# Loading x in 128-partition halves: one padded transfer in place of 112 partitions and a last row

## The chip, the cores and the metric

The kernel runs on one core of one Trainium2 chip. Time is the device time of one execution in microseconds (us). The engines are TensorE (PE; its weight loads are shown as PEld), VectorE (DVE), ScalarE (ACT), GpSimd (POOL) and SyncE (SP). SP computes nothing: in this kernel it issues nearly all transfers between device memory and SBUF, in the order in which its program lists them, and 16 DMA engines carry them out.

## What is computed

```python
def _attn_ref(x, filt_r, filt_i):            # x: 8 x 3136 x 256
    X = np.fft.rfft(x, axis=1)
    F = (filt_r + 1j * filt_i)[None, :, :]
    return np.fft.irfft(X * F, n=x.shape[1], axis=1)
def _moe_ref(x, w_gate, w1, w2, capacity):   # x: what _attn_ref gave; capacity 128
    scores = np.einsum('bsd,d->bs', x, w_gate)
    out = x.copy()
    for b in range(B):
        top_idx = np.argpartition(-scores[b], capacity)[:capacity]
        xe = x[b, top_idx]
        ye = np.maximum(xe @ w1, 0.0) @ w2
        g = 1.0 / (1.0 + np.exp(-scores[b, top_idx]))
        out[b, top_idx] = xe + g[:, None] * ye
```

Each of the 8 batches is filtered along its 3136 positions in the frequency domain; the 128 positions of each batch with the highest scores then get a small feed-forward network.

## The kernel before

The Fourier transforms are matmuls: 3136 = 98 x 32, and the 98 rows are cut in two groups of 49 (`NH`). A batch lies in the SBUF tile `X` (partitions x 2 channel halves x 2 x 16 x 128 floats): group 0 in partitions 0 to 48, group 1 in partitions 64 to 112. So 113 partitions hold data or the zeros between the groups, each with 16 KB in one channel half. All compute on `X` works on `64 + NH` = 113 partitions.

`X` is one buffer for all batches, and its life in the steady state is a cycle. `fold` (L489, on POOL or DVE) makes sum and difference of the two middle indices, or the sum is left to PE; `amm` (L500, on PE) multiplies; `tout` (L505, DVE) transposes the product into `UU`. `inner` then filters the batch (L376 to L441). When batch t+1 has been consumed from `X`, the results of batch t-1 are written into the same place by `join` (L541) or `yout` (L567), `store_rows` (L579, L580) sends that half to device memory in six transfers, and `load` (L594, L595) brings that half of batch t+2 in. A load thus has to wait until the six stores of its half have been read out, and the folds of the next batch wait for the load.

`load` is called for 14 halves (batches 1 to 7), and issues two transfers for each: first the row of partition 112, 16 KB cut in 16 pieces (L594), then partitions 0 to 111 (L595). `load_first` does the same for batch 0, in four quarters with 8 KB in a partition (L608, L609). The host lays x out for that: per batch the 112 rows of both halves one behind the other, then the last rows.

The order of all work is written out as a list of numbers (`ORDER`), and every engine runs its part in that order; SP's part is the order of transfers. The transfers of SP go round eight completion semaphores ("lanes"), so a transfer may be issued only when the one eight places earlier has landed.

Of the kernel before, what the change touches and what calls it, by code (L numbers as in the profile page):

```python
# [18 lines left out]
B, S, D, FF = 8, 3136, 256, 1024  # L19
N1, N2, K2, L, LP = 98, 32, 32, 25, 32  # L20
NH, NG = 49, 16
# [233 lines left out]
def kernel(  # L255
# [7 lines left out]
    nc = tc.nc  # L263
# [61 lines left out]
    def op(when, eng, cost, fn, r=(), w=(), new=None, lat=0.0, bias=0.0, sooner=0.0, mode=0, tag=None):  # L325

        prog.append((when, len(prog), eng, cost, fn, r, w, new, (tag or fn.__name__, *where)))
# [129 lines left out]
    halves = [c_sb[:, _COLS["wi"].start + NH * k:_COLS["wi"].start + NH * k + 64] for k in range(2)]  # L457
# [121 lines left out]
                nc.sync.dma_start(out=oi[b, g, :48, h, :, d], in_=X[64 * g:64 * g + 48, x, h])  # L579
            nc.sync.dma_start(out=oi[b, :, 48, h, :, d], in_=X[48::64, x, h])  # L580

    XM = 2 * 112 * 4096

    def load(when, b, h, xy, bias=0.0):
        n = NCH // 2
        where[:] = "ld", b, h
        if b < B:
            keys = [("x", h, c, g) for c in range(h * n, h * n + n) for g in range(2)]
            to = X[:, h].rearrange("p k n d -> p (k n d)")
            main = x[b, :XM].rearrange("(h p e) -> h p e", h=2, p=112)  # L590
            ends = x[b, XM:].rearrange("(r h e) -> h r e", h=2, r=16)

            def fetch():
                nc.sync.dma_start(out=to[112:113].rearrange("p (r e) -> p r e", r=16), in_=ends[h:h + 1])  # L594
                nc.sync.dma_start(out=to[:112], in_=main[h])  # L595

            op(when, "sp", 7.15, fetch, [], keys, lat=2.2, bias=bias, tag="load")

    x_flat = X.rearrange("p x k n d -> p (x k n d)")
    x_first = x_flat.rearrange("p (q k n d) -> p q k n d", q=4, k=2, n=NG)  # L600

    def load_first():
        main = x[0, :XM].rearrange("(q p e) -> q p e", q=4, p=112)
        ends = x[0, XM:].rearrange("(r q e) -> q r e", q=4, r=16)

        def quarter(q):
            to = x_flat[:, 2048 * q:2048 * q + 2048]
            nc.sync.dma_start(out=to[112:113].rearrange("p (r e) -> p r e", r=16), in_=ends[q:q + 1])  # L608
            nc.sync.dma_start(out=to[:112], in_=main[q])  # L609

        for q in range(4):
            keys = [("x", q // 2, 4 * q + c, g) for c in range(4) for g in range(2)]
            op(XQ[q], "sp", 3.7, lambda q=q: quarter(q), [], keys, lat=2)
# [528 lines left out]
    if WARM:  # L1142
        op(-99.5, "pe", .117 * WARM, warmup, (), (), new=("y", "warm"))
        for _ in range(FILL):
            op(-99.4, "pe", .64, fill, (), [("y", "warm")])
    op(-99, "sp", .4, lambda: nc.sync.dma_start(out=c_sb[:, :192], in_=cst[:, :192]), (), ["wa"], lat=2)
    load_first()
    for k, (a, e) in enumerate(((0, 4 * CUT), (4 * CUT, L))):
        op(TFT[k], "sp", .25 + .125 * (e - a), lambda a=a, e=e: nc.sync.dma_start(out=tf_sb[:, a:e], in_=tf.rearrange("p (l c) -> p l c", c=64)[:, a:e]),
# [34 lines left out]
    for h in range(2):  # L1184
        load(TS + TC0 * NCH / 2 * (h + 1) + 1, 1, h, xys[1], XA)
    for t in range(B + 1):
        T0 = t * P if t < B else (B - 1) * P + C8
        if t < B:
            if t == 0:
                inner(I0, P - I0, t)  # L1190
            else:
                inner(T0, P if t < B - 1 else P7, t)
        co, tc_ = (CO, TCO) if t < B - 1 else (C7, TC7) if t == B - 1 else (0, .95)
        outer(T0 + co, tc_, t - 1, t + 1, xys[t + 1])
        if t + 2 < B + 2:
            for h in range(2):
                load(T0 + co + tc_ * NCH / 2 * (h + 1) + (6 if t < B - 1 else 4), t + 2, h, xys[t + 2])
        if t >= 1:
            select(T0 + SO if t < B else T0 - C8 + S7, t - 1, sts[t - 1])
# [45 lines left out]
```

## Time and profile before

| | |
|---|---|
| median of 3 runs | 459.41 us (453.93 to 1026.87) |
| profiled execution | 455.47 us |
| its span (first to last instruction) | 453.7 us |
| PE busy | 416.2 us (92%) |
| DVE busy | 355.8 us (78%) |
| POOL busy | 328.2 us (72%) |
| ACT busy | 313.0 us (69%) |
| DMA, mean over the span | 152 GB/s |
| granted TensorE clock, mean | 0.972 |

The rows further down are from the profiled execution. Busy time of PE is that of overlapping matmuls, so 92% does not say that it runs at its peak. "L595" is line 595 of the kernel. `<-` in a pair of names reads "written from". A number in square brackets with `<-` behind an instruction is the time its engine sat idle before it and what ended that.

### The profile page before, as it was taken

Reading aid. Unit: us, or ns where it says so; the run is one execution under the profiler, and the core shown is the slowest. Engines: PE = TensorE matmul, PEld = TensorE weight load, DVE = VectorE, ACT = ScalarE, POOL = GpSimd, SP = SyncE. Lnnn points to the kernel's source line nnn. Section 1 sums busy time; section 2 is a strip of 40 time slices with the busy share of each in tenths; the row PEclk is TensorE's granted clock in tenths of the full one; section 3 lists DMA queues with packets and bytes.
Section 4 is the critical chain, followed back from the end, with each engine's and each line's share of the span. In section 5 each row is a group of like instructions: output and inputs, shape, how many; then the busy total and the mean of one; then the engine's idle time right before and its main releaser. Section 6 shows DMA issues by size and latency. Waiting matters only on the chain.

```text
span 453.7 us, 13314 instructions
## 1 busy us (share of the span) xinstructions
PE 416.2 (92%) x5348; PEld 249.7 (55%) x5348; DVE 355.8 (78%) x711; ACT 313.0 (69%) x798; POOL 328.2 (72%) x215
## 2 busy tenths in 40 slices
PE   9999999999699998979999799989999979998884
PEld 9644565545354644535555454456545756577773
DVE  2568899989869898995889698979899985964421
ACT  1429947789268977984989397948988997852210
POOL 2317799797969588867998589539889995964121
PEclk9999999999889999997999899989999989999999
DMA  8999973058654757584747563675253791566100
GB/s 230 256 258 277 243 175 92 8 138 226 163 124 111 207 136 201 144 211 110 212 103 196 152 200 91 183 183 161 63 125 96 181 267 27 131 154 151 39 25 35
DMA packets 61548, 69.05 MB, mean 152 GB/s; under 512 B 4014, under 2 KB 57550, under 8 KB 59214
## 3 DMA queue, kind: packets, MB, share of 16 engines
q1 hardware_dynamic: 60718, 66.10, 57.0%
q0 software_dynamic: 768, 2.10, 1.5%
q8 instruction: 42, 0.69, 0.6%
q14 instruction: 20, 0.16, 0.1%
HBM read 41.27 MB, written 26.91 MB: 150 GB/s over the span
## 4 chain that ended last, share of the span: by engine, by line
PE 42%; DMA 18%; DVE 15%; POOL 10%; ACT 9%; issue 4%; SPq 1%; POOLq 0%; ACTq 0%; DVEq 0%
DMA X<-in_x_dram 9%; PE pv L500 4%; DVE t L479 4%; ACT junk L441 4%; POOL q L435 3%; DMA fb_sb<-in_fri_dram 3%; PE pv L1006 3%; DVE y L384 3%; POOL xh L489 3%; PE py L400 3%; PE pa L500 3%; DMA out_dram<-X 2%; DVE q L391 2%; PE pa L1034 2%; DVE UU L505 2%
## 5 line engine op out<-in xcount | busy, mean ns | idle before, releaser
L435 POOL TENSOR_TENSOR q<-UU,wg_sb 128x1024 f32<-128x1024 f32 (+1 forms) x47 | 109.1, 2327 | 11.7 <-ACT UU L408 5.0
L541 POOL TENSOR_TENSOR X<-xh,X 113x512 f32<-113x512 f32 x64 | 81.7, 1287 | 18.5 <-ACT X L537 14.1
L441 ACT ACTIVATE junk<-q 128x256 bf16<-128x256 f32 x180 | 75.1, 417 | 13.2 <-POOL q L435 8.1
L479 DVE STREAM_TRANSPOSE t<-UU 128x1024 f32<-128x1024 f32 x64 | 78.0, 1224 | 0.0
L489 POOL TENSOR_TENSOR xh<-X 113x512 f32<-113x512 f32 x26 | 34.7, 1341 | 24.1 <-DMA X<-in_x_dram 24.1
L387 POOL TENSOR_TENSOR q<-q,fb_sb 128x1024 f32<-128x1024 f32 (+1 forms) x18 | 40.6, 2254 | 11.9 <-ACT q L380 11.7
L489 POOL TENSOR_TENSOR X<-X 113x512 f32<-113x512 f32 x24 | 31.2, 1302 | 13.2 <-DMA fa_sb<-in_fri_dram 7.0
L500 PE MATMUL pv<-X,c_sb 49*64 49x512 f32 x184 | 33.7, 709 | 7.1 <-DMA X<-in_x_dram 4.0
L441 ACT ACTIVATION_READ_ACCUMULATOR junk<-q 128x1 f32 x180 | 33.9, 188 | 0.0
L726 ACT ACTIVATE junk<-R,nb 128x392 bf16<-128x392 f32 (+1 forms) x48 | 30.0, 626 | 4.9 <-DVE nb L747 4.2
L505 DVE STREAM_TRANSPOSE UU<-pv 128x1024 f32<-128x1024 f32 x19 | 23.6, 1240 | 10.0 <-PE pv L500 9.9
L500 PE MATMUL pa<-X,c_sb 49*64 49x512 f32 x192 | 30.0, 596 | 0.5 <-DVE UU L505 0.5
L505 DVE STREAM_TRANSPOSE UU<-pa 128x1024 f32<-128x1024 f32 x21 | 25.9, 1233 | 5.4 <-PE pa L500 5.4
L1018 ACT ACTIVATE q<-pv 128x384 fp32r<-128x384 f32 (+2 forms) x18 | 8.0, 457 | 29.8 <-PE pv L1006 21.3
L1020 DVE SCALAR_TENSOR_TENSOR y<-pv,q 128x384 fp32r<-128x384 f32 (+2 forms) x18 | 9.0, 511 | 24.3 <-ACT q L1018 19.3
L384 DVE TENSOR_TENSOR y<-pa,fa_sb 128x1024 f32<-128x1024 f32 (+1 forms) x19 | 22.5, 1186 | 3.8 <-PE pa L376 2.9
L500 PE MATMUL py<-X,c_sb 49*64 49x512 f32 x168 | 24.0, 592 | 0.0
L563 PE MATMUL pz<-t,c_sb 64*64 64x512 f32 x160 | 23.1, 618 | 0.5 <-ACT X L567 0.5
L400 PE MATMUL py<-y,ti_sb 64*64 64x256 f32 x252 | 21.7, 396 | 0.7 <-DVE y L384 0.7
L376 PE MATMUL pa<-UU,tf_sb 64*64 64x256 f32 x292 | 21.2, 395 | 0.9 <-DMA tf_sb<-in_tf_dram 0.2
L400 PE MATMUL py<-q,ti_sb 64*64 64x256 f32 x252 | 21.1, 386 | 0.0
L1046 POOL DMA_INDIRECT out_dram<-fb_sb,idx_sb x6 | 5.9, 980 | 20.3 <-DVE fb_sb L1042 12.9
(340 smaller groups left out, 1144.8 us busy)
## 6 DMA issues: line engine op xcount, KB each, us to landing
X<-in_x_dram SPq DMA_DIRECT2D x14, 1792.0 KB
out_dram<-X SPq DMA_DIRECT2D x64, 384.0 KB
X<-in_x_dram SPq DMA_DIRECT2D x4, 896.0 KB
R<-scr SPq DMA_DIRECT2D x14, 196.0 KB
fb_sb<-in_moe_w_dram SPq DMA_DIRECT2D x2, 1024.0 KB
fa_sb<-in_fri_dram SPq DMA_DIRECT2D x4, 256.0 KB
fb_sb<-in_fri_dram SPq DMA_DIRECT2D x4, 256.0 KB
ti_sb<-in_ti_dram SPq DMA_DIRECT2D x1, 576.0 KB
```

What stands on the lines that cost most here:

```text
L384: nc.vector.tensor_tensor(out=wide(y), in0=wide(h["z"]), in1=filt(fa_sb), op=ALU.mult)
L387: nc.gpsimd.tensor_tensor(out=wide(h["q"]), in0=wide(h["q"]), in1=filt(fb_sb), op=ALU.mult)
L400: nc.tensor.matmul(v[o, j, c], lhsT=ti_at[p, k, 2 * i + e, hi], rhs=y[p, hi, c], start=k == 0, stop=k == 1)
L435: nc.gpsimd.tensor_tensor(out=h["q"][:, e0:e0 + ne].rearrange("p e (j d) -> p e j d", j=2), in0=u.rearrange("p e d j -> p e j d"), in1=wg_ ...
L441: nc.scalar.activation(out=rk, in_=h["q"][:, e, j * D:j * D + D], func=AF.Copy, accum_out=urow(b, ls[2 * e + j], D, DS))
L479: nc.vector.transpose(out=h["t"].rearrange("p d (l j) -> p d l j", j=2), in_=uchan(b_out, c))
L489: eng.tensor_tensor(out=(area(1) if k else h["f"])[:64 + NH], in0=area(0)[:64 + NH], in1=area(1)[:64 + NH], op=(ALU.add, ALU.subtract)[k])
L500: nc.tensor.matmul(ap[64 * k:64 * k + 64, g].rearrange("p (n d) -> p n d", d=DW), lhsT=todo[k][i][0][p], rhs=todo[k][i][1][p], start=i == ...
L505: nc.vector.transpose(out=uchan(b_in, c), in_=a.rearrange("p (l j) d -> p d l j", j=2))
L541: eng.tensor_tensor(out=area(k)[:64 + NH], in0=h["e"][:64 + NH], in1=odd, op=(ALU.add, ALU.subtract)[k])
L563: nc.tensor.matmul(h["y"][64 * g:64 * g + 64, k], lhsT=halves[k][p], rhs=h["t"][p, :, NG * g:NG * g + NG], start=turn == 0, stop=turn == 1)
L726: nc.scalar.activation(out=junk, in_=st["R"][:, ph], func=AF.Sign, bias=st["nb"], accum_out=cnt)
```

## The change

x is laid out by the host with 128 partitions for each half of a batch (partitions 49 to 63 and 113 to 127 are zeros), and each half is fetched by one transfer of 128 partitions x 16 KB. Batch 0's quarters likewise are one transfer of 128 partitions x 8 KB. No compute instruction changes; `X` already had 128 partitions, of which the last 15 were not written before and are not read afterwards.

```diff
-    XM = 2 * 112 * 4096
-
     def load(when, b, h, xy, bias=0.0):
...
-            main = x[b, :XM].rearrange("(h p e) -> h p e", h=2, p=112)
-            ends = x[b, XM:].rearrange("(r h e) -> h r e", h=2, r=16)
+            main = x[b].rearrange("(h p e) -> h p e", h=2, p=128)

             def fetch():
-                nc.sync.dma_start(out=to[112:113].rearrange("p (r e) -> p r e", r=16), in_=ends[h:h + 1])
-                nc.sync.dma_start(out=to[:112], in_=main[h])
+                nc.sync.dma_start(out=to, in_=main[h])
...
     def load_first():
-        main = x[0, :XM].rearrange("(q p e) -> q p e", q=4, p=112)
-        ends = x[0, XM:].rearrange("(r q e) -> q r e", q=4, r=16)
+        main = x[0].rearrange("(q p e) -> q p e", q=4, p=128)

         def quarter(q):
-            to = x_flat[:, 2048 * q:2048 * q + 2048]
-            nc.sync.dma_start(out=to[112:113].rearrange("p (r e) -> p r e", r=16), in_=ends[q:q + 1])
-            nc.sync.dma_start(out=to[:112], in_=main[q])
+            nc.sync.dma_start(out=x_flat[:, 2048 * q:2048 * q + 2048], in_=main[q])
...
-    padded = np.zeros((B, 2, 64 + NH, 4096), np.float32)
-    padded[:, :, :NH], padded[:, :, 64:] = halves[:, :, 0], halves[:, :, 1]
...
+    padded = np.zeros((B, 2, 128, 4096), np.float32)
+    padded[:, :, :NH], padded[:, :, 64:64 + NH] = halves[:, :, 0], halves[:, :, 1]
```

Only SP's program changes. Here is SP in the steady state, from the stores of one half of batch 0 to the load of batch 3 that takes their place, before. `DMAHW0` to `DMAHW7` are the eight lanes; a wait on a compute engine's name is a wait for its work.

```order
L579 DMA out_dram<-X 48x16x128 [waits DMAHW2_49,DVE_49,DMAHW3_49,Activation_49,Pool_49]
L579 DMA out_dram<-X 48x16x128
L580 DMA out_dram<-X 32x1x128 [waits DMAHW4_49]
L579 DMA out_dram<-X 48x16x128 [waits DMAHW5_49,Pool_49]
L579 DMA out_dram<-X 48x16x128 [waits DMAHW6_49]
L580 DMA out_dram<-X 32x1x128
L594 DMA X<-in_x_dram 1x16x256 [waits DMAHW4_49,DMAHW7_49,DMAHW0_49,PE_49]
L595 DMA X<-in_x_dram 112x4096 [waits DMAHW5_49,DMAHW3_49,DMAHW6_49,DMAHW2_49,DMAHW1_49]
```

And the same place in the changed kernel:

```order
L579 DMA out_dram<-X 48x16x128 [waits DMAHW2_49,DVE_49,DMAHW4_49,Activation_49,Pool_49]
L579 DMA out_dram<-X 48x16x128
L580 DMA out_dram<-X 32x1x128
L579 DMA out_dram<-X 48x16x128 [waits DMAHW5_49,Pool_49]
L579 DMA out_dram<-X 48x16x128 [waits DMAHW6_49]
L580 DMA out_dram<-X 32x1x128
L591 DMA X<-in_x_dram 128x4096 [waits DMAHW4_49,DMAHW5_49,DMAHW3_49,DMAHW6_49,DMAHW2_49,DMAHW7_49,DMAHW0_49,PE_49]
```

The two transfers, of which the first waited for the short stores (L580) and the second for the long ones (L579), are one that waits for all six. The other place is SP near the start, where batch 1's second half and batch 2's first are fetched behind the filter's tables, before:

```order
L1149 DMA tf_sb<-in_tf_dram 128x1088 [waits DMAHW2_49]
L1151 DMA wg_sb<-in_moe_w_gate_dram 128x256 [waits DMAHW3_49]
L1100 DMA fa_sb<-in_fri_dram 32x1536 [waits DMAHW4_49]
L1100 DMA fa_sb<-in_fri_dram 32x1536 [waits DMAHW5_49]
L1100 DMA fb_sb<-in_fri_dram 32x1536 [waits DMAHW6_49]
L1100 DMA fb_sb<-in_fri_dram 32x1536 [waits DMAHW7_49]
L594 DMA X<-in_x_dram 1x16x256 [waits DMAHW0_49,PE_49,Pool_49]
L595 DMA X<-in_x_dram 112x4096 [waits DMAHW1_49]
L594 DMA X<-in_x_dram 1x16x256 [waits DMAHW2_49,PE_49,Pool_49]
L595 DMA X<-in_x_dram 112x4096 [waits DMAHW3_49]
```

And in the changed kernel (its lines 1093, 1142 and 1144 are 1100, 1149 and 1151 of before):

```order
L1142 DMA tf_sb<-in_tf_dram 128x1088 [waits DMAHW5_49]
L1144 DMA wg_sb<-in_moe_w_gate_dram 128x256 [waits DMAHW6_49]
L1093 DMA fa_sb<-in_fri_dram 32x1536 [waits DMAHW7_49]
L1093 DMA fa_sb<-in_fri_dram 32x1536 [waits DMAHW0_49]
L1093 DMA fb_sb<-in_fri_dram 32x1536 [waits DMAHW1_49]
L1093 DMA fb_sb<-in_fri_dram 32x1536 [waits DMAHW2_49]
L591 DMA X<-in_x_dram 128x4096 [waits DMAHW3_49,PE_49,Pool_49]
L591 DMA X<-in_x_dram 128x4096 [waits DMAHW4_49,PE_49,Pool_49]
```

The order of the transfers stays; the small ones drop out, so the lane that each transfer waits for is that of another predecessor.

## Rows read from the trace of the kernel before

**Rows 1.** The page's chain that ended last, by engine and the first lines.
```profile
PE 42%; DMA 18%; DVE 15%; POOL 10%; ACT 9%; issue 4%; SPq 1%; POOLq 0%; ACTq 0%; DVEq 0%
```

**Rows 2.** The chain in order of time: start us, us, what.
```profile
40.43 13.90 DMA X<-in_x_dram
...
144.53 6.12 DMA out_dram<-X
...
150.71 9.13 DMA X<-in_x_dram
...
192.75 0.60 SPq L594
...
193.53 9.98 DMA X<-in_x_dram
203.65 3.66 PE pv L500 x14
...
288.38 9.65 DMA X<-in_x_dram
298.16 2.95 PE pv L500 x16
```

**Rows 3.** DMA issues: names, engine, count, KB of each.
```profile
X<-in_x_dram SPq DMA_DIRECT2D x14, 1792.0 KB
X<-in_x_dram SPq DMA_DIRECT2D x4, 896.0 KB
fb_sb<-in_moe_w_dram SPq DMA_DIRECT2D x2, 1024.0 KB
X<-in_x_dram SPq DMA_DIRECT2D x14, 16.0 KB
X<-in_x_dram SPq DMA_DIRECT2D x4, 8.0 KB
```

**Rows 4.** Windows: stretch, busy us (x instructions) of each engine, clock, DMA share, GB/s.
```profile
25.00:54.00 29.00, 28.43 (x384) 15.21 (x376) 24.13 (x28) 19.49 (x24) 16.55 (x10) 1.00 1.01 257
153.00:157.00 4.00, 4.00 (x70) 2.69 (x64) 4.00 (x6) 3.16 (x11) 3.92 (x3) 1.00 1.03 307
195.00:200.00 5.00, 4.72 (x72) 2.22 (x64) 4.87 (x15) 4.87 (x14) 2.93 (x2) 1.00 0.90 272
290.00:295.00 5.00, 4.46 (x76) 2.30 (x72) 4.93 (x15) 4.84 (x18) 2.57 (x2) 1.00 1.00 279
345.50:347.50 2.00, 1.96 (x36) 1.04 (x35) 1.89 (x9) 1.97 (x5) 1.92 (x3) 1.00 0.99 406
```

**Rows 5.** Timeline of SP: start us, us of the issue, line and names.
```profile
150.71 0.35 SPq L595 DMA_DIRECT2D X<-in_x_dram  x1
192.75 0.60 SPq L594 DMA_DIRECT2D X<-in_x_dram  x1
193.53 0.44 SPq L595 DMA_DIRECT2D X<-in_x_dram  x1
287.60 0.59 SPq L594 DMA_DIRECT2D X<-in_x_dram  x1
288.38 1.09 SPq L595 DMA_DIRECT2D X<-in_x_dram  x1
343.45 0.42 SPq L923 DMA_DIRECT2D fb_sb<-in_moe_w_dram  x1
```

**Rows 6.** Timeline of POOL, then PE: instructions that waited for a load [idle us <-releaser].
```profile
111.78 1.30 POOL L489 TENSOR_TENSOR xh<-X 113x512 f32<-113x512 f32 x1 [1.81 <-DMA X<-in_x_dram]
159.97 1.27 POOL L489 TENSOR_TENSOR xh<-X 113x512 f32<-113x512 f32 x1 [2.97 <-DMA X<-in_x_dram]
253.15 1.28 POOL L489 TENSOR_TENSOR xh<-X 113x512 f32<-113x512 f32 x1 [4.17 <-DMA X<-in_x_dram]
54.46 0.66 PE L500 MATMUL pz<-X,c_sb 49*64 49x512 f32 x4 [0.48 <-DMA X<-in_x_dram]
203.65 1.13 PE L500 MATMUL pv<-X,c_sb 49*64 49x512 f32 x4 [2.11 <-DMA X<-in_x_dram]
298.16 1.24 PE L500 MATMUL pv<-X,c_sb 49*64 49x512 f32 x8 [1.88 <-DMA X<-in_x_dram]
```

More of the change, by code (lines that the diff above doesn't have):

```diff
@@ L1226 @@
     halves = rows_of.reshape(B, 2, NH, 2, NG, 2, D // 2).transpose(0, 5, 1, 2, 3, 4, 6).reshape(B, 2, 2, NH, 4096)
-    padded = np.zeros((B, 2, 64 + NH, 4096), np.float32)
-    padded[:, :, :NH], padded[:, :, 64:] = halves[:, :, 0], halves[:, :, 1]
-    first = padded[0].reshape(2, 64 + NH, 2, NG, 2, 64).transpose(0, 4, 1, 2, 3, 5).reshape(4, 64 + NH, 2048)
-    data["x"] = np.concatenate([padded[:, :, :112].reshape(B, -1), padded[:, :, 112].reshape(B, 2, 16, 256).transpose(0, 2, 1, 3).reshape(B, -1)], 1)
-    data["x"][0] = np.concatenate([first[:, :112].reshape(-1), first[:, 112].reshape(4, 16, 128).transpose(1, 0, 2).reshape(-1)])
+    padded = np.zeros((B, 2, 128, 4096), np.float32)
+    padded[:, :, :NH], padded[:, :, 64:64 + NH] = halves[:, :, 0], halves[:, :, 1]
+    data["x"] = padded.reshape(B, -1).copy()
+    data["x"][0] = padded[0].reshape(2, 128, 2, NG, 2, 64).transpose(0, 4, 1, 2, 3, 5).reshape(-1)
     data.update(fri=np.stack([np.asarray(inputs[f"filt_{x}"])[rows].reshape(64, NPR, 2, D) for x in "ri"]), tf=tf.reshape(128, -1), ti=ti, cst=cst)
```

## Prediction

> **What bounds the kernel now.** I read the chain that ended last first. No engine owns it: PE has 42%, and transfers have 18%, more than DVE or POOL [rows 1]. The reader should see that a kernel whose PE is 92% busy still stands still for transfers. Then I took the chain in order of time to find which transfers those are. Loads of x stand in it four times, with 13.90, 9.13, 9.98 and 9.65 us from issue to landing [rows 2], together 42.66 us. They have two surroundings. The first, at 40.43, lies in the head of the program, where the tables and the first batches come in and the DMA engines are full (share 1.01 from 25 to 54 us, [rows 4]); its 13.90 us are mostly a queue. The other three are in the steady state: stores of a half end, SP issues the load that takes their place, and PE or POOL waits for it. I then asked the timelines who waits: PE sat idle 2.11 us before 203.65 and 1.88 us before 298.16, POOL 2.97 us before 159.97 [rows 6]. These waits are small against 9 to 10 us of transfer, since other work covers most of each load. What a faster load can give is capped by them, while a slower load costs in full.
>
> **The change part by part.** It has three parts.
>
> *The small transfer goes.* In 18 places (14 halves, 4 quarters, [rows 3]) SP issues one transfer in place of two. At 192.75 and 287.60 the small one was issued first and the large one 0.78 us later [rows 5]. If all stores have landed by then, the one transfer starts at the small one's time: 0.78 us sooner. The bounds are 0 and 0.78, since a long store that still landed under the small issue holds the one transfer up. I take 0.78. At 150.71 it gives nothing: the store that was issued at 144.53 landed at 144.53 + 6.12 = 150.65 and the load followed at once [rows 2], so the merged one starts there too. All six stores are waited for either way, and behind the load on SP stand only the next stores and the score transfers, which gain. The lanes that change hands have predecessors eight transfers back; I cost them at nothing because in the steady state these have landed long before, and if one had not, the load would wait up to a store's 6.12 us.
>
> *Bytes are added.* A load is 1792 + 16 = 1808 KB now and 2048 KB then; a quarter 904 and 1024 KB.
>
> *The shape changes, 112 partitions to 128.* This decides the sign, and the trace before has no 128 x 16 KB transfer, so I bound it. While a 112-partition load runs with little beside it, the DMA engines move 307, 272 and 279 GB/s, at a share of 0.90 to 1.03: they are busy and yet slow [rows 4]. The 1835008 bytes of 1792 KB then need 5.98, 6.75 and 6.58 us of the 9.13, 9.98 and 9.65, which leaves 3.15, 3.23 and 3.07 us for start and landing; I use 3.1. The only large 128-partition transfer that runs alone is the weight load that is issued at 343.45 [rows 5], 1024 KB [rows 3] in pieces of 4 KB: 406 GB/s, at a share of 0.99 [rows 4]. So 128 partitions can be faster per byte by a third or more. For the new load, 2097152 bytes: at 406 GB/s 5.17 + 3.1 = 8.27 us; at 272 to 307 GB/s 6.83 to 7.71, in all 9.9 to 10.8 us. I take 406, because the transfer is like the new one in the partitions that it spans, which is what the change alters; what speaks for the other end is that its rows are 4 KB and those of x are 16 KB.
>
> The Trainium skill, page "SBUF — State Buffer", section "Door 1: The DMA port swizzle", says that a transfer's bandwidth depends on which of 16 ports its partitions reach, and that each port serves eight of the 128 partitions. By its table 112 partitions leave four ports with four rows and twelve with eight, so a transfer held by its fullest port would take as long for 112 as for 128: the streaming would cost nothing and gain nothing. By that rule the sum is only the two 0.78 us, 453.9 us, and it is a rival below. The trace agrees as far as that 128 partitions run faster per byte, but 406 against 272 to 307 GB/s is more than the rule's 128/112.
>
> **The sum,** by place:
> - 150.71: 9.13 becomes 8.27, 0.86 us sooner; POOL's wait was 2.97, so all of it counts.
> - 193.53: 9.98 becomes 8.27, and 0.78 from the issue: 2.49, capped by PE's wait of 2.11. I count 2.1.
> - 288.38: 9.65 becomes 8.27, and 0.78: 2.16, capped by 1.88. I count 1.9.
> - Head: at 54.46 PE waited only 0.48 [rows 6]. Four quarters and batch 1's two halves carry 4 x 120 + 2 x 240 = 960 KB more than before. If all six go at 406 GB/s, their 8.39 MB take 20.7 us, while the 7.41 MB of before at the head's 257 GB/s take 28.8: far more than can be used. If the queue stays at 257 GB/s, the 983040 extra bytes cost 3.8 us. I take the near end of the gain, capped: 0.5.
>
> In all 0.86 + 2.1 + 1.9 + 0.5 = 5.4 us. The loads that end the waits at 111.78 and 253.15 [rows 6] also get shorter, but they do not stand in the chain; I count nothing for them. What is late next: after 203.65 and 298.16 the chain is PE itself [rows 2], so PE's own order carries the gain on. From the profiled execution's 455.47 us (span 453.7 and 1.8 us around it) that gives 450.1. The median of the three runs shown, 459.41, is 0.9% above the profiled one and their lowest, 453.93, 0.3% below; I forecast from the profiled one.
>
> **The rivals.**
>
> *A, slower: rows keep their price.* If a 16 KB row costs what it does now, because the limit is on the memory's side and not on the partitions, an eighth more bytes go at the old rates. Then 262144 bytes (of 2048 against 1792 KB) cost 0.85, 0.96 and 0.94 us at the three places; less the 0.78 us where the issue comes sooner: 0.85 + 0.18 + 0.16, and the head's 3.8, in all +5.0: 460.5 us. For it: three different loads lie close together at 272 to 307 GB/s, and the head, which mixes shapes, at 257. Against it: the same DMA engines gave 406. The first place turns from gain to loss at 2.10 MB / (9.13 - 3.1) = 348 GB/s. If the longer loads also drop to the head's 257 GB/s, each is 8.16 + 3.1 = 11.3 us: +2.1, +0.5, +0.8 and 3.8: 462.7 us.
>
> *B, nothing to see.* Streaming costs as much as before (the port rule above, 453.9), or the loads get shorter and the freed engine waits for DVE (78% busy) or ACT at once. For it: most of each load is already hidden. Against: PE's waits name only the load. Time 453.5 to 456.5; I put 454.5.
>
> *C, more than forecast.* POOL's waits at 111.78 (1.81) and 253.15 (4.17) matter after all, since folds feed PE some steps later. If they give back about the same as the places above, 1.5 and 2.5 us, it is 4 us more: 446 us. Against: these waits are not in the chain.
>
> **How the numbers follow.** Forecast (447 to 453): 0.47. B (453 to 457): 0.2. A (457 to 463): 0.2. C (443 to 447): 0.13. Predicted is the likeliest, 450.1 us. The range leaves out about half of C and the far end of A, under 2 in 10: 445 to 461.5. About 2% is what a measurement of this kernel can tell from no change, that is below 446.4 or above 464.6 against the profiled time. C's lower part is faster by that, 0.1; and if the median of before is again as high as 459.41, to which I give one chance in three, 450.1 is 2% below it and the forecast's 0.47 counts too: 0.25 in all. A's far end with further contention in the head is slower: 0.07. Same: 0.68.
>
> **What would show it.** In the profile of the changed kernel the stretches just after the loads' start should read near 400 GB/s at a share near 1, and the loads in the chain 8 to 8.5 us; 270 to 310 GB/s and 10 to 11 us would be rival A. PE's waits on the loads near 203 and 298 should be under 0.5 us; if they are gone and the time is the same, it is B, and the wait that follows them names the cause. The load after the stores near 192 and 287 should be issued where the small one was. The prediction is wrong in its main step if a 128-partition transfer with 16 KB rows does not come near 406 GB/s, and wrong in its caps if the time falls by more than the waits counted here.

## The result and the profile after

The changed kernel takes 437.3 us (median of 4 runs, 434.79 to 438.04). The kernel before took 459.6 us beside it (4 runs, of which one of 1026.87 us is disturbed). The ratio is 0.9545 with a 95% interval of 0.9446 to 0.9644. A ratio, here and below, leaves out runs more than 1.5% above the fastest of the same kernel; medians and ranges are of all runs. The prediction said 450.1 us and at best 445: the sign was right, the size was not. The profiled execution took 436.59 us with a span of 434.8, which is 18.9 us less than the 453.7 of before.

The page of the kernel after: busy time, granted clock in 40 slices, chain by engine, transfers of x.

```profile
PE 407.3 (94%) x5348; PEld 247.3 (57%) x5348; DVE 357.5 (82%) x711; ACT 312.9 (72%) x798; POOL 329.0 (76%) x215
...
PEclk9999999999999999999999999999999999999997
...
PE 32%; DVE 19%; POOL 18%; ACT 11%; issue 10%; DMA 6%; SPq 1%; POOLq 0%; ACTq 0%; DVEq 0%
...
X<-in_x_dram SPq DMA_DIRECT2D x14, 2048.0 KB
X<-in_x_dram SPq DMA_DIRECT2D x4, 1024.0 KB
```

Transfers fell from 18% of the chain to 6% [rows 1]. The only load of x that is left in the chain, in order of time:

```profile
188.13 8.81 DMA X<-in_x_dram
```

Windows of the kernel after (stretch, busy us and instructions of PE, PEld, DVE, ACT, POOL, clock, DMA share, GB/s), the last three early in a load:

```profile
25.00:54.00 29.00, 28.26 (x380) 15.30 (x384) 23.27 (x28) 17.89 (x21) 16.71 (x11) 1.00 0.95 333
190.00:193.00 3.00, 3.00 (x54) 1.62 (x48) 2.93 (x8) 2.87 (x12) 2.44 (x1) 1.00 0.88 371
236.00:239.00 3.00, 2.29 (x52) 1.49 (x48) 3.00 (x4) 2.76 (x11) 2.92 (x3) 1.00 1.02 431
277.00:281.00 4.00, 3.45 (x56) 1.64 (x56) 3.93 (x10) 3.87 (x16) 2.57 (x2) 1.00 0.94 397
```

So the main step held: where 112 partitions moved 307, 272 and 279 GB/s [rows 4], 128 move 371 to 431, and the load in the chain takes 8.81 us where 9.98 and 9.65 stood [rows 2]. Two others, issued at 232.83 and 274.32, had landed when PE started on them at 241.22 and 282.75 (rows below), so they took at most 8.4 us.

**Where the 18.9 us went, by PE.** The span is PE's busy time plus its idle time. Busy time fell from 416.2 us to 407.3, by 8.9, with the same 5348 instructions; idle time fell by the other 10.0. The idle time shows in the timelines. PE after, the instructions that waited at 203.65 and 298.16 in [rows 6], with three others:

```profile
119.80 0.30 PE L806 MATMUL pa<-rc,c_sb 64*64 64x2 f32 x7 [1.98 <-DVE ge L788]
...
197.08 1.51 PE L500 MATMUL pv<-X,c_sb 49*64 49x512 f32 x11 [0.54 <-DMA X<-in_x_dram]
...
241.22 1.09 PE L500 MATMUL pv<-X,c_sb 49*64 49x512 f32 x8 [0.60 <-DMA X<-in_x_dram]
...
282.75 1.52 PE L500 MATMUL pv<-X,c_sb 49*64 49x512 f32 x12
...
351.08 1.10 PE L1027 MATMUL pa<-fb_sb 128*128 128x256 f32 x4
```

And these three in the kernel before:

```profile
121.47 0.42 PE L813 MATMUL pa<-rc,c_sb 64*64 64x2 f32 x8 [3.90 <-DVE ge L795]
...
253.15 1.09 PE L500 MATMUL pv<-X,c_sb 49*64 49x512 f32 x8 [3.15 <-DVE vs L631]
...
370.06 1.48 PE L1034 MATMUL pa<-fb_sb 128*128 128x256 f32 x4 [2.19 <-DMA fb_sb<-in_moe_w_dram]
```

The busy time shows in the clock. Windows of PE in the kernel before (stretch, PE busy, clock, DMA share, GB/s), at the end of the five longest waits or up to 1.4 us behind it:

```profile
121.47:128.30 6.83, 6.41 (x56) 0.50 1.01 254
...
203.39:210.20 6.81, 6.55 (x44) 0.50 0.74 179
...
254.59:258.00 3.41, 3.41 (x36) 0.50 0.62 155
...
298.97:302.40 3.43, 3.43 (x28) 0.50 0.78 183
...
370.65:374.00 3.35, 3.35 (x10) 0.50 0.92 242
```

PE ran at the lower of its two levels (1.2 instead of 2.4 GHz) for 23.8 us, each time after a wait of 1.88 to 3.90 us. (Below, such a stretch is called a fall.) The same stages of the kernel after are at the upper level throughout; it falls only in its last 10 us. It has the wait of 1.98 us at 119.80 and no fall behind it. So waits are shorter or gone, and with them the falls of the clock behind them. Two of the five places are no plain gain: the wait at 370.06 is for a weight load, and a fall at the selection (121.47) comes back in kernels below that are as fast as this one.

### The profile page after: what moved, and what is told of

Its sections match the earlier page's. It is cut to its first block, busy times and chain, and to the rows that moved or that the text cites. A ratio compares the mean times of both kernels' runs of the same rounds, so it can differ in the third digit from the quotient of the medians.

```text
span 434.8 us, 13274 instructions
## 1 busy us (share of the span) xinstructions
PE 407.3 (94%) x5348; PEld 247.3 (57%) x5348; DVE 357.5 (82%) x711; ACT 312.9 (72%) x798; POOL 329.0 (76%) x215
## 4 chain that ended last, share of the span: by engine, by line
PE 32%; DVE 19%; POOL 18%; ACT 11%; issue 10%; DMA 6%; SPq 1%; POOLq 0%; ACTq 0%; DVEq 0%
POOL X L541 6%; POOL q L435 6%; ACT junk L441 4%; DVE UU L505 4%; DMA out_dram<-X 4%; DVE y L384 4%; DVE t L479 3%; PE pv L999 3%; DVE q L391 2%; PE pv L500 2%; PE pa L500 2%; POOL xh L489 2%; PE py L1111 2%; POOL X L489 2%; DMA X<-in_x_dram 2%
## 5 line engine op out<-in xcount | busy, mean ns | idle before, releaser
L441 ACT ACTIVATE junk<-q 128x256 bf16<-128x256 f32 x180 | 75.2, 418 | 10.2 <-POOL q L435 5.4
L500 PE MATMUL pv<-X,c_sb 49*64 49x512 f32 x184 | 28.9, 597 | 1.3 <-DMA X<-in_x_dram 1.1
L563 PE MATMUL pz<-t,c_sb 64*64 64x512 f32 x160 | 22.2, 595 | 0.5 <-ACT X L567 0.5
L400 PE MATMUL py<-y,ti_sb 64*64 64x256 f32 x252 | 20.8, 380 | 0.7 <-DVE y L384 0.7
```

Source lines behind the costliest of these rows:

```text
L400: nc.tensor.matmul(v[o, j, c], lhsT=ti_at[p, k, 2 * i + e, hi], rhs=y[p, hi, c], start=k == 0, stop=k == 1)
L441: nc.scalar.activation(out=rk, in_=h["q"][:, e, j * D:j * D + D], func=AF.Copy, accum_out=urow(b, ls[2 * e + j], D, DS))
L500: nc.tensor.matmul(ap[64 * k:64 * k + 64, g].rearrange("p (n d) -> p n d", d=DW), lhsT=todo[k][i][0][p], rhs=todo[k][i][1][p], start=i == ...
L563: nc.tensor.matmul(h["y"][64 * g:64 * g + 64, k], lhsT=halves[k][p], rhs=h["t"][p, :, NG * g:NG * g + NG], start=turn == 0, stop=turn == 1)
```

## Experiments

Two questions. Is it the shape that makes the load faster, and which loads matter? And how did waits of 2.1 and 1.9 us become 18.9 us: was it the clock, or loads that the prediction had counted at nothing? Ratios are to runs of before on the same chip, which had medians of 452.16 to 454.47 us.

**The same bytes in two transfers.**

```diff
-                nc.sync.dma_start(out=to, in_=main[h])
+                nc.sync.dma_start(out=to[112:], in_=main[h, 112:])
+                nc.sync.dma_start(out=to[:112], in_=main[h, :112])
```

> The changed kernel, with the halves of batches 1 to 7 fetched in two transfers again: partitions 112 to 127, then 0 to 111, of the same padded x. Bytes and the host's layout are those of the changed kernel, the large transfer's partitions those of before. Theory S (the shape: a transfer over 128 partitions runs faster than one over 112, the waits of PE on loads shrink with it, and the stretches at half clock that follow those waits go): loads 9 to 10 us again, waits of PE of 2 us and more again, half-clock stretches again, 450 to 460 us. Rival L (the layout in memory: with rows at a multiple of 128 x 16 KB the memory serves the loads faster, whatever partitions they go to): loads stay at 8 to 9 us, 436 to 442 us.

457.35 us, ratio 1.0099 [1.0033, 1.0166]. The layout, the bytes and the number of rows are those of the kernel after, and the whole gain is gone. (The 16 partitions are issued some 0.5 us ahead of the 112; what an issue ahead is worth is tried below, about 1%.) Two loads from its chain in time, and a window (all engines) in the first of them:

```profile
197.08 10.20 DMA X<-in_x_dram
...
292.97 10.58 DMA X<-in_x_dram
```
```profile
199.00:204.00 5.00, 4.49 (x72) 2.21 (x64) 4.87 (x14) 4.87 (x15) 3.16 (x2) 1.00 0.91 252
```

A transfer of 112 partitions, with the 16 just ahead of it, takes 10.2 us also out of the padded layout, and the DMA engines move 252 GB/s.

**Halves of 64 partitions.**

```diff
-                nc.sync.dma_start(out=to, in_=main[h])
+                nc.sync.dma_start(out=to[:64], in_=main[h, :64])
+                nc.sync.dma_start(out=to[64:], in_=main[h, 64:])
```

> The changed kernel, with each half of a batch as two transfers of 64 partitions, 0 to 63 and 64 to 127; bytes and layout are those of the changed kernel. If what makes 128 partitions fast is that one transfer spans all of them, each of the two runs at about half the rate and a half of a batch takes 12 us or more: 460 to 480 us. If it is only the number of rows that each DMA engine gets (a multiple of 4 in place of 7), it stays at 8 to 9 us: 437 to 442 us.

467.66 us, ratio 1.03 [1.0226, 1.0374]. From its chain in time, the second transfer of two halves:

```profile
204.73 11.95 DMA X<-in_x_dram
...
255.68 12.04 DMA X<-in_x_dram
```

and windows in these loads:

```profile
206.00:213.00 7.00, 6.34 (x92) 2.89 (x88) 6.85 (x17) 6.50 (x17) 5.07 (x3) 1.00 1.03 225
258.00:265.00 7.00, 6.28 (x108) 3.87 (x107) 6.84 (x14) 6.27 (x20) 6.25 (x4) 1.00 1.00 208
```

The DMA engines are busy all the time at about half of the 431 GB/s of one transfer. The Trainium skill, page "DMA: Bandwidth & Descriptors", section "Rules for kernel authors", says that two transfers to disjoint halves of the partitions serialize and that one of 128 should be used instead; 12 us against 8.81 in the chain agree that nothing is won, and here it is a loss.

The traces hold every packet of the DMA engines, and a row of 16 KB is one packet. Its median time in the last ten loads was 0.61 us in each of them with 128 partitions (after), 0.86 to 1.09 with 112 (before), 0.90 to 1.03 with 112 and 16, and 1.25 to 1.29 with twice 64. The windows agree: 371 GB/s at a share of 0.88 are 26.3 GB/s for each of the 16 engines, 16 KB in 0.62 us; 272 at 0.90 [rows 4] are 18.9, in 0.87 us. So a load on fewer partitions is slow because each packet takes longer, while the engines stay busy. What makes a packet longer is not shown.

**A second issue, and its place.** After, with 16 KB fetched into an unused tile ahead of each load; and before, with its two transfers in the other order:

```diff
+                nc.sync.dma_start(out=spare, in_=x[b, :4096].rearrange("(r e) -> r e", r=16))
                 nc.sync.dma_start(out=to, in_=main[h])
```

> The changed kernel, with a small transfer (16 KB in 16 rows of 1 KB, into a tile that nothing reads) ahead of each of the 14 loads, as before the change; the loads stay 128 partitions wide. Theory S (shape): the issue costs about 0.7 us a load, partly covered: 437 to 441 us. Rival I (what was taken away counts: the second issue, its lane and its landing): 448 to 456 us.

437.21 us, ratio 0.9665 [0.9609, 0.9722], no different from after. Another small transfer that waits for nothing in `X` costs nothing: in the trace one is issued at 185.31 and its load at 188.53, so its issue falls into the load's wait for the stores.

```diff
-                nc.sync.dma_start(out=to[112:113].rearrange("p (r e) -> p r e", r=16), in_=ends[h:h + 1])
                 nc.sync.dma_start(out=to[:112], in_=main[h])
+                nc.sync.dma_start(out=to[112:113].rearrange("p (r e) -> p r e", r=16), in_=ends[h:h + 1])
```

> The kernel before, with the large transfer of each half issued before the small one. Rival I (the second issue ahead of the load costs 0.7 us a load, and PE falls for it): 1 to 2% faster. Theory S (shape): the issue is a small part, under 1% faster, and the last row may land later than before.

449.41 us, ratio 0.9894 [0.9835, 0.9954]: 1% from the order of two lines. The large transfer no longer stands behind the 0.6 to 0.8 us of the small one [rows 5]. That alone is close to what was forecast for the whole change. Part of it may be the clock: in its trace PE waits 1.38 and 2.35 us for x, before 205.59 and 294.41, and the clock stays at 1.00 behind both.

**Which loads.** After, with batch 0's quarters as before:

```diff
...
         def quarter(q):
-            nc.sync.dma_start(out=x_flat[:, 2048 * q:2048 * q + 2048], in_=main[q])
+            to = x_flat[:, 2048 * q:2048 * q + 2048]
+            nc.sync.dma_start(out=to[112:113].rearrange("p (r e) -> p r e", r=16), in_=ends[q:q + 1])
+            nc.sync.dma_start(out=to[:112], in_=main[q])
```

> The changed kernel with batch 0's four quarters fetched as before (112 partitions and a last row); only the 14 halves are 128-partition transfers. If the gain is that of the loads in the steady state and of the clock that they keep up: 436 to 440 us. If a good part came from the head (quarters that land sooner): 442 to 450 us.

438.46 us, ratio 0.9677 [0.9615, 0.9739]: all of it without the quarters. The other way round, before with only the quarters changed:

```diff
...
         def quarter(q):
-            to = x_flat[:, 2048 * q:2048 * q + 2048]
-            nc.sync.dma_start(out=to[112:113].rearrange("p (r e) -> p r e", r=16), in_=ends[q:q + 1])
-            nc.sync.dma_start(out=to[:112], in_=main[q])
+            nc.sync.dma_start(out=x_flat[:, 2048 * q:2048 * q + 2048], in_=main[q])
```

> The kernel before, with batch 0's four quarters as 128-partition transfers; the 14 halves stay 112 partitions and a last row. By the run with only the halves changed, which reached the time of the whole change, the head should bring nothing: within 1% of the kernel before. If the two parts overlap in what they bring, it would be 1 to 2% faster alone.

Its four runs lie between 440.68 and 453.05 us, too far apart for a ratio. Their median, 448.82, is 5.3 us below the 454.14 of before, so a gain from the quarters alone is not excluded; once the halves are changed, the quarters add nothing that shows.

Then the fourteen halves in two ways. `fetch` takes the one transfer where a condition holds and the two of before elsewhere:

```diff
+                if h == 0 and b in (4, 5, 7):      # then its negation, then h == 0, then h == 1
                     nc.sync.dma_start(out=to, in_=main[h])
+                else:
+                    nc.sync.dma_start(out=to[112:113].rearrange("p (r e) -> p r e", r=16), in_=ends[h:h + 1])
+                    nc.sync.dma_start(out=to[:112], in_=main[h, :112])
```

> The three loads that stood in the chain of before in the steady state (h = 0 of batches 4, 5 and 7, issued at 149.69, 192.75 and 287.60 there) are loaded in one transfer on 128 partitions; the other eleven steady halves go as 112 partitions and a last row, as before; batch 0's quarters stay on 128. Theory 'only the chain counts' (that of the prediction, with its caps lifted): the time is near that of the full change, 438 to 441 us. Theory 'every load counts' (X is one buffer in a cycle of load, transform, store, and each load's length is in it): 3/14 of the gain of 15.5 us, 3.3 us, so 449 to 451 us if before is at 453. The two differ by 10 us.

> The complement: the eleven steady halves that did not stand in the chain of before go on 128 partitions in one transfer, the three of the chain (h = 0 of batches 4, 5, 7) as 112 partitions and a last row. 'Only the chain counts': next to no gain, 450 to 453 us. 'Every load counts': 11/14 of 15.5 us, 12.2 us, so 440 to 442 us if before is at 453. A gain near that of the full change in both this and its complement would mean that the two sets stand in for each other.

> Only the seven halves h = 0 of batches 1 to 7 go on 128 partitions; the seven halves h = 1 as 112 partitions and a last row. 'Every load counts', both halves alike: half the gain, 445 to 446 us if before is at 453. A cycle that goes through one half alone: all of it here (437 to 439 us) or nothing (452 to 453). 'Only the chain counts': all three loads of the chain are h = 0, so 438 to 441 us.

> Only the seven halves h = 1 of batches 1 to 7 go on 128 partitions; the seven halves h = 0 as 112 partitions and a last row. 'Every load counts', both halves alike: 445 to 446 us if before is at 453. A cycle through h = 0 alone, or 'only the chain counts': 451 to 453 us. A cycle through h = 1 alone: 437 to 439 us.

| | median, us | runs | ratio to before |
|---|---|---|---|
| three of the chain | 447.39 | 441.75 to 451.99 | 0.9853 [0.9554, 1.0152] |
| the other eleven | 443.59 | 437.85 to 445.68 | 0.9793 [0.9421, 1.0164] |
| h = 0 only | 438.87 | 438.29 to 440.6 | 0.9757 [0.9607, 0.9908] |
| h = 1 only | 449.06 | 442.04 to 452.46 | 0.9879 [0.9528, 1.0229] |

Only the third ratio excludes 1; what the other three sets give alone is not resolved. But every run with h = 0 only is faster than every run with h = 1 only, and than every run with the three of the chain. The seven halves h = 0 give all the gain within 1.6 us, so "every load counts" is wrong for h = 1, which adds next to nothing on top of them. The three of the chain do not give all of it (some 7 us by the medians), so "only the chain counts" is wrong too. PE's waits show why. In the kernel with the three of the chain:

```profile
203.43 1.09 PE L500 MATMUL pv<-X,c_sb 49*64 49x512 f32 x8 [0.99 <-DMA X<-in_x_dram]
...
250.65 0.66 PE L500 MATMUL pv<-X,c_sb 49*64 49x512 f32 x4 [3.66 <-DMA X<-in_x_dram]
```

and with the other eleven:

```profile
199.31 1.09 PE L500 MATMUL pv<-X,c_sb 49*64 49x512 f32 x8 [1.66 <-DMA X<-in_x_dram]
...
286.14 1.09 PE L500 MATMUL pv<-X,c_sb 49*64 49x512 f32 x8 [1.85 <-DMA X<-in_x_dram]
```

Where a load is left slow, PE waits for it: at 250.65 for batch 6, whose wait the profile of before put down to DVE; at 199.31 and 286.14 for batches 5 and 7. A half h = 0 is needed as soon as it lands. A half h = 1 lands while PE works on h = 0: in before, PE has no idle time over 0.3 us that ends on the loads issued at 216.66, 264.56 and 311.55.

**The clock.** Dummy products ahead of the first product of h = 0 fill PE's wait and take the clock's fall away, while the loads stay slow:

```diff
+                for _ in range(fillers):
+                    nc.tensor.matmul(ap[:64, 0, :256], lhsT=c_sb[:, :64], rhs=c_sb[:, 192:448], start=True, stop=True)
                 todo = [[(wa[i][k], area(i)) for i in range(2)] ...
```

In the first run the fillers of the three waits were not in the program, by a mistake, and eight others, at the selection of batch 0, stood behind the wait at L813 that they were to fill.

> The kernel before, with matmuls of constants put on PE ahead of four places where it stood idle (8 ahead of the counts in the selection of batch 0; 4, 7 and 4 ahead of the first product of batches 5, 6 and 7), each of 64 x 256 into a bank that the real matmuls overwrite. Loads are untouched. Theory C (about half of the gain is the clock: PE that waited 1.9 to 3.9 us fell to half clock for 3.4 to 6.8 us, 20.5 us in all at these four places): PE does not fall there, 445 to 450 us. Rival W (the gain is that of the waits alone, and the half-clock stretches were covered by other work): 453 to 457 us.

456.28 us, ratio 1.0075 [1.002, 1.013]; it tells nothing of the three waits. With 7, 10 and 6 of them in batches 5, 6 and 7:

> The kernel before, with 7, 10 and 6 matmuls of constants (64 x 256) at the head of the first product of batches 5, 6 and 7, the three places where PE stood idle for a load (2.1, 3.2 and 1.9 us) and then went at half clock for 6.8, 3.4 and 3.4 us. Loads are untouched. In the first try at this the fillers of these three places were not in the program, and those of the selection stood behind its wait. Theory C (the half clock costs by itself): PE does not fall at these three places, and 13.6 us at half clock, up to 6.8 us of work, are saved: 446 to 450 us where the kernel before has 452 to 456. Rival W (only the waits count): no change, or 1 to 2 us slower where fillers overrun.

451.84 us, ratio 0.9955 [0.9906, 1.0005]. The falls at the three places were gone, but the fillers were too many. The one group of 14 pieces (7 fillers) in its timeline of PE, ahead of a load that had landed before they ended:

```profile
203.90 3.24 PE L496 MATMUL pv<-c_sb 128*64 128x256 f32 x14
207.07 1.95 PE L502 MATMUL pv<-X,c_sb 49*64 49x512 f32 x16
```

3.24 us stand in place of a wait of 2.11. So, with 3, 5 and 3:

> Before, with 3, 5 and 3 dummy products (64 x 256, about 0.47 us each in the run with 7, 10 and 6 of them) ahead of the first product of h = 0 in batches 5, 6 and 7, where TensorE waited 2.11, 3.15 and 1.88 us for x. They fill 1.4, 2.4 and 1.4 us of these waits and leave under a microsecond of each; the loads stay as they were. In before, the clock fell to half right after these waits. 'Half of the gain is the clock': the falls at the three places go, TensorE is 7 us less busy at what it did before, and the time falls by 5 to 7 us, to 447 to 449 us if before is at 454. 'The clock is next to nothing, the loads' length is all': 453 to 455 us.

451.09 us over 12 runs, ratio 0.9874 [0.9824, 0.9925], that is 5.7 us less (1.26% of 454.18). Its page, its timeline of PE and two windows of PE:

```profile
PE 412.5 (92%) x5370; PEld 245.2 (55%) x5370; DVE 356.6 (80%) x711; ACT 313.1 (70%) x798; POOL 328.8 (74%) x215
```
```profile
202.93 1.51 PE L496 MATMUL pv<-c_sb 128*64 128x256 f32 x6
204.62 1.95 PE L502 MATMUL pv<-X,c_sb 49*64 49x512 f32 x16 [0.17 <-DMA X<-in_x_dram]
```
```profile
203.00:210.00 7.00, 6.83 (x87) 1.00 0.82 188
...
296.00:300.00 4.00, 4.00 (x72) 1.00 0.68 158
```

The clock stays at 1.00 behind a load that is as slow as before. Without the 22 pieces at 0.23 us PE is busy 407.4 us, as in the kernel after. The two medians differ by 3.1 us only; I read the gain as 3 to 6 us. The twelve runs fall in two groups, six of 445.35 to 449.68 us at a mean clock of 0.989 to 0.996 and six of 452.51 to 455.69 at 0.983 to 0.988. The trace is of the first group and has one fall before the last 10 us, behind the selection; where the clock fell in the others is not known.

**What a microsecond of PE costs there.** After, with the 7, 10 and 6 fillers:

> After (437 us), with 7, 10 and 6 of the same dummy products at the same three places, 10.8 us of TensorE's time where it waits only 0.54, 0.60 and 0 us. It prices TensorE's own time in these stages, by what a halved clock would cost: if each microsecond of TensorE counts in full, 446 to 448 us; if other engines' work covers it (the time is set by the cycle of load, folds and stores), 438 to 441 us.

445.2 us, ratio 0.9812 [0.9756, 0.9868], 7.9 us above the 437.3 of after. The same group in its timeline of PE:

```profile
197.66 3.23 PE L496 MATMUL pv<-c_sb 128*64 128x256 f32 x14
200.83 1.95 PE L502 MATMUL pv<-X,c_sb 49*64 49x512 f32 x16
```

46 pieces at 0.23 us are 10.6 us of fillers; less the waits of 0.54 and 0.60 that they cover, 9.5 us. So a microsecond of PE costs 7.9 / 9.5 = 0.8 us of time at these three places. In before, PE was busy there for 6.55, 3.41 and 3.43 us at half clock, 13.4 us for what takes 6.7 at the upper level; the other 6.7 are then about 5 us of time, an estimate that the light fillers' 3 to 6 us bear out.

That price does not hold everywhere. The kernel with the small transfer into an unused tile has PE's wait behind the selection as after has it, but with a fall behind it (a row of its timeline of PE, a window of PE):

```profile
119.02 0.30 PE L808 MATMUL pa<-rc,c_sb 64*64 64x2 f32 x7 [1.97 <-DVE ge L790]
```
```profile
121.54:124.95 3.41, 3.41 (x24) 0.50 1.01 432
```

Its profiled execution took 436.44 us, that of after, without this fall, 436.59: here a fall cost nothing that shows.

**Still shorter loads.**

```diff
-                nc.sync.dma_start(out=to, in_=main[h])
+                nc.sync.dma_start(out=to[:, :2048], in_=main[h, :, :2048])
```

> After, with the first 8 KB of each partition's 16 KB loaded for the fourteen halves of batches 1 to 7 (the rest of x stays unread, and what is left in the buffer is used in its place). A load should take 5.2 to 5.8 us in place of 8.15 (2.6 us of streaming less). 'The length of the loads still counts in full': at the 2.2 us per h = 0 load of the runs before, 437 - 7 x 2.6 = 419 us. 'The gain is used up, since TensorE waits for x only some 0.5 us at two places in after and no fall of the clock is left to remove': 434 to 437 us.

437.83 us, ratio 0.9652 [0.96, 0.9705]: no faster than after. (The 8.15 us of the expectation stand in no row; the loads of h = 0 in after that can be timed took 8.3 to 8.8.) Not every load became as short as expected: in the last ten the last packet ended 5.0 to 8.2 us after the issue, against 7.7 to 10.7 in after (a load here waits only for the stores of what it overwrites, so it is issued sooner and can run beside others). But none of PE's waits names a load of x any more. With the waits gone, faster loads give nothing; what sets the 437 us then, with PE 94% busy in after, was not tested.

## Why the prediction was wrong

| term | forecast | PE's row before, after | measured |
|---|---|---|---|
| load at 193.53 | 2.1 | 2.11, 0.54 | 1.6 |
| load at 288.38 | 1.9 | 1.88, none | 1.9 |
| load at 150.71 | 0.86 | no wait of PE for it | not seen |
| head | 0.5 | batch 2's h = 1 load issued at 61.54, 62.06 | nothing on top of the halves |
| wait of POOL at 253.15 | 0 | 3.15, 0.60 | 2.6 |
| wait of POOL at 111.78 | 0 | 3.90, 1.98 (behind DVE) | 1.9 |
| clock behind the waits | not thought of | busy 416.2, 407.3 | 8.9 busy; 3 to 6 of time at three places |

**Right:** the shape decides the sign. The forecast of 8.27 us for a load came from a transfer of 128 partitions with 4 KB rows; measured were 8.81 in the chain, at most 8.4 for two others, and 371 to 431 GB/s, so rival A (rows keep their price) fell, and the run with 112 and 16 partitions shows that bytes and layout have no part in it. The rule on ports of the Trainium skill (page "SBUF — State Buffer", section "Door 1: The DMA port swizzle"), rival B, read as a bound by the fullest port, would have made 112 partitions as fast as 128; here 112 took 9.13 to 10.2 us and 128 took 8.81, so the measurement decides against that reading. By the same section partitions 0 to 63, like 64 to 127, reach eight of the 16 ports, half of them; the 208 to 225 GB/s of 64 partitions against 431 of 128 agree. The caps of 2.1 and 1.9 us at the two loads were right in size too.

**The step that failed** is the sum. It was built on the two waits of PE that name the load, and rival B was held down because "PE's waits name only the load"; PE's two longest waits, 3.90 and 3.15 us, name DVE. First: "they do not stand in the chain; I count nothing for them." PE's waits that hung on these loads became 1.9 and 2.6 us shorter. The chain goes one way back at each instruction, and where PE's wait was put down to DVE, the chain left the load. At 253.15 PE and POOL start in the same moment, and POOL had waited 4.17 us for the load [rows 6]. The kernel with the three of the chain shows it: PE's wait at that place then names the load. At 111.78 the way is longer: POOL waited 1.81 us for the load [rows 6], and then DVE for POOL, shortly before the selection on which PE waited 3.90 us:

```profile
117.12 2.86 DVE L489 TENSOR_TENSOR X<-X 113x512 f32<-113x512 f32 x1 [1.18 <-POOL xh L489]
```

In the traces in which that load was on 128 partitions the wait at the selection is 1.95 to 1.98 us, in those with the slow load 2.27 us and more. That was rival C, with 0.13.

Second, and of about the same size: the caps priced a wait at its own length. A wait of 2 us was followed by up to 6.8 us of PE at half clock. The windows of [rows 4] were laid on the loads, and all of them show a clock of 1.00; windows a few microseconds later would have shown 0.50, and the mean of 0.972 stood in the table. PE's busy time in the five falls, 23.1 us, would be 11.6 at the upper level; 8.9 of the difference are in the profile, and the light fillers give back 3 to 6 us of time at three of the five places. The prediction had named the sign: its caps are wrong if the time falls by more than the waits counted.

Waits of x at PE are 6.1 us (1.6, 1.9 and 2.6), the wait behind the selection 1.9, each counted at its own length, and the clock at the three places 3 to 6. Together they make 11 to 14 of the 15 us by which the medians differ on the chips of the experiments (437.2 to 438.5 against 452 to 454). Where the rest comes from is not shown; the falls behind the selection and the weight load, longer in before than in any kernel of 437 to 439 us, are one candidate. The 18.9 us of the two profiled executions hold 2.19 us for the second weight load besides. I claim no part for it: the run with half the bytes had a wait of that size again (1.98 us before 352.10) and the same time.

**Open:** why 112 partitions stream at 252 to 307 GB/s, that is, why a packet of 16 KB takes 0.86 to 1.09 us in place of 0.61. Neither bytes, layout nor a second issue explains it, and how rows are dealt to the DMA engines was not tried.

## What to carry to other kernels

Where a load is waited for, try to give it all 128 partitions in one transfer, even if an eighth of it is padding, and issue nothing ahead of it that its first user doesn't need. When you price a wait of PE, look at the granted clock behind it, since a short wait can cost more than its length, and check whether DVE or POOL had waited for the same transfer before you cost a load outside the chain at nothing. When PE no longer waits for the transfer, stop: here still shorter loads gave nothing.

## What was not expected of the hardware

- Time by the shape of 2048 KB with 16 KB rows: 128 partitions 8.81 us in the chain; 112 and 16 partitions 10.2 to 10.6 us for the 112; twice 64 partitions 12 us for the second. The engines were busy in all three (shares of 0.88 to 1.03); a packet of 16 KB took 0.61, about 1.0 and 1.27 us.
- The time of before goes with the granted clock from run to run: over 44 runs on four chips from 447.46 us at a mean clock of 0.992 to 462.31 us at 0.969; a straight line through all of them falls by 5.4 us per 0.01. At after's 0.994 it gives 446 us, still 9 us above after. The kernel after, without waits that bring the clock down, varied by 3 us.
- Before the last 10 us of a kernel, falls stood at the end of waits of PE of 1.85 us and more, or behind them (the 1.85 at 286.14 in the kernel with the other eleven had half clock from 287.39 to 290.80), but not behind each: after's 1.98 us brought none, nor did 2.63 us, before 203.03, in the kernel with only the quarters changed.
